# Scores of two groups in one burst, values one tile sooner and a transpose half a tile later, in a fused chunk attention and squared-ReLU FFN on one core

## The chip, the cores and the metric

One Trainium2 chip, of which the kernel uses 1 core. The metric is the device time of one execution in microseconds (us), as the median of several runs. The core's engines run side by side, each with a queue of its own: TensorE (PE) for matmuls and for transposes against an identity, VectorE (DVE), ScalarE (ACT) and GpSimd (POOL) for elementwise work, and SyncE (SP), which issues most DMAs. They wait for each other through semaphores. Loading PE's weights shows as a row of its own, PEld.

## The reference

Attention inside chunks of 64 tokens, for 8 batches, 8 heads, 576 tokens and a head size of 64; then a feed-forward layer with a squared ReLU (d_model 512, d_ff 2048) over all 4608 tokens.

```python
# q_c, k_c, v_c: q, k, v cut into chunks of 64 tokens
scores = scale * np.matmul(q_c, k_c.transpose(0, 1, 2, 4, 3))
scores = scores - np.max(scores, axis=-1, keepdims=True)
attn = np.exp(scores)
attn = attn / (np.sum(attn, axis=-1, keepdims=True) + 1e-09)
out = np.matmul(attn, v_c)
x = np.ascontiguousarray(attn_out.transpose(0, 2, 1, 3)).reshape(B * S, H * D)
h = np.maximum(x @ w_in, 0.0)
return (h * h @ w_out).astype(np.float32)
```

## The kernel before

**Groups and blocks.** 256 tokens (four chunks) are a group; there are 18 groups. Two groups are a block of 512 tokens: block j holds groups 2j and 2j + 1, so block 1 holds groups 2 and 3, and block 4 groups 8 and 9. The feed-forward layer runs block by block, and during block j the attention of block j + 1 is slipped in between. (Block 0 prepares only group 2 of block 1; group 3 is prepared in block 1 itself.) Blocks 0 to 3 (`QUADS = 4`) multiply by w_in in the plain way; from block 4 on, matrix sums save products.

**The attention of a group** has four steps, each a function that issues on several engines.
- q and k are brought into a transposed layout, by PE (`transpose_qk`, L393 with the copies of L402) or, for later groups, cast to bf16 (L442, L447) and transposed by a DMA that SP issues (L453).
- `scores` (`SC`): 32 matmuls of 64 x 64 into one PSUM buffer of two banks (L476), and one ACT exp of 128 x 1024 out of it (L487).
- `values` (`AV`): for each of the group's two token tiles, 16 matmuls of 64 x 65 into a PSUM buffer (L503); a column of ones in v gives the sum of the weights. DVE takes its reciprocal (L435) and multiplies the result by it (L436), writing x.
- `transpose_x` (`XT`): eight PE transposes of x (L533) and one copy from PSUM to `xT` (L538), by ACT for most groups, group 3 among them.

All these take their PSUM buffers from `att_bank`, which in blocks 0 to 3 hands out two buffers by turns, `ps_att` and `ps_att2`. In block 3 the order is: scores 8, scores 9, values 8 (two buffers), values 9 (two), x of 8, x of 9. So the two halves of the values of group 9 write the buffers out of which DVE normalised the two halves of group 8, and PE waits for DVE's last read of each.

**The feed-forward part** is `ffn_in` (L572 to L591). A d_ff tile is 128 rows of d_ff for the tokens at hand: four matmuls into one of four `ps_ffn` buffers, a ReLU by ACT into one of four `relu_sb` buffers (L583), and a square into `gT`, by DVE (L591) or, for the tiles in `SQUARES_ON_ACT = (10, 14, 3)`, by ACT (L589). In blocks 2 and 3 a tile has 512 tokens and 16 tiles follow each other. In block 1 a step is half as wide, 256 tokens: steps 0 to 15 work on group 2 and steps 16 to 31 on group 3, so step 16 is the first to read the x of group 3. `ffn_out` (L773) then multiplies by w_out, with sums by DVE (L607).

**Order.** The schedule is written by hand (`manual_schedule`): each engine runs its instructions in the order in which the program issues them. For blocks 0 to 3 the loop goes through the phases of a block, and each `yield` of a phase ends a slot. Slot s comes behind d_ff tile s (block 1: half tile s); from slot 16 on (block 1: 32) slots lie in `ffn_out`. In a slot, one load is issued if the slot is among `go_slots`, and then whatever `plan` holds for the slot, in the order in which it was put there by `at(slot, f, group)`. The loads of v, q and k go through SP; their slots are in lists of their own, and no load is tied to an attention step's slot.

From block 4 on (`run(tick)`) the order goes by ticks, with lists of the same kind.

Of the kernel before, what the change touches and what calls it, by code (L numbers as in the profile page):

```python
# [144 lines left out]
def kernel(  # L145
# [169 lines left out]
    def go(pieces):  # L315
        for f in pieces:
            f()
# [248 lines left out]
    def ffn_in(j, parts):  # L566
        gT = gT_main.rearrange("p (u h) (f t) -> p u h f t", u=2, f=4)
        xT = xTs[j]
        for u, (c, n, ft) in enumerate((c, n, ft) for c, n, fts in parts for ft in fts):
            h = ps_ffn.tile([128, 512], FP32, name="ps_ffn")  # L570
            for dt in range(n_dt):
                nc.tensor.matmul(  # L572
                    out=h[:, 0:n],
                    lhsT=w_in_bf[:, dt, ft * 128:(ft + 1) * 128],
                    rhs=xT[:, c // 128:(c + n) // 128, dt, :],
                    start=(dt == 0), stop=(dt == n_dt - 1))
            if n == 512 or u % 2 == 0:
                state["rl"] = state.get("rl", -1) + 1
                rl_tile = relu_sb[state["rl"] % 4]
                if j < 3:  # L580
                    rl_tile = rl_tile.bitcast(BF16)
            rl = rl_tile[:, u % 2 * 512:] if n < 512 else rl_tile
            nc.scalar.activation(out=rl[:, 0:n], in_=h[:, 0:n], func=AF.Relu)  # L583
            u0, u1 = c // GT, (c + n) // GT
            dst = gT[:, u0:u1, ft // 4, ft % 4, :]
            src = rl[:, 0:n].rearrange("p (u t) -> p u t", t=GT)
            if (n == 512 and ft in SQUARES_ON_ACT) or (
                    n < 512 and ft in (12, 3)) or (j == 0 and u == 0):
                nc.scalar.activation(out=dst, in_=src, func=AF.Square)  # L589
            else:  # L590
                nc.vector.tensor_tensor(out=dst, in0=src, in1=src, op=ALU.mult)  # L591
            yield
# [16 lines left out]
    def summed(out, in0, in1, op=ALU.add):  # L609
        return lambda *_: add(out, in0, in1, op)  # L610
# [274 lines left out]
    def ffn_out_by_ft(j):  # L885

        n_tt = BT // 128
        o_ps = [ps_ffn.tile([128, d_model], FP32, name="ps_ffn") for _ in range(n_tt)]

        def mm(tt, ft):  # L890
            nc.tensor.matmul(  # L891
                out=o_ps[tt],
                lhsT=g_piece(j, tt // 2, ft // HF, ft % HF // 4)[
                    :, ft % 4, tt % 2 * 128:tt % 2 * 128 + 128],
                rhs=w_out_bf[:, ft, :],
                start=(ft == 0), stop=(ft == n_ft - 1))


        for ft in range(n_ft - 4):
            for tt in range(n_tt - 1 if ft == 0 else n_tt):  # L900
                mm(tt, ft)
                if ft == 1 and tt == n_tt - 2:
                    mm(n_tt - 1, 0)
            yield
        for tt in range(n_tt):
            for ft in range(n_ft - 4, n_ft):
                mm(tt, ft)
            o_sb = ffn_pool.tile([128, d_model], FP32, name="o_sb", bufs=4)
            nc.scalar.copy(out=o_sb, in_=o_ps[tt])
            b, s0 = chunks[blocks[j][tt // 2]][0]  # L910
            t0 = b * S + s0 + tt % 2 * 128
            nc.gpsimd.dma_start(out=out[t0:t0 + 128, :], in_=o_sb)
            yield
# [3 lines left out]
    def pieces(grps):  # L917
        for g in grps:
            yield from qk_pieces(g)
        for g in grps:  # L920
            yield from v_pieces(g)

    SC, AV, XT = scores, values, transpose_x
    TD = transpose_qk_dma
# [71 lines left out]
    for j in range(QUADS):  # L996
        grps, nxt, far = blocks[j], blocks[j + 1], blocks[j + 2]
        plan = {}

        def at(slot, f, *x):  # L1000
            plan.setdefault(slot, []).append((f, x))

        if j == 0:
            loads, go_slots = pieces(far), range(17)
            at(28, summed(b11_p_b21, b11, b21))
            for slot, f in ((24, TA), (27, SC), (29, AV), (31, XT)):
                at(slot, f, nxt[0])
            at(31, TQ, nxt[1])
            at(31, TK, nxt[1])
            at(31, summed(b22_m_b21, b22, b21, ALU.subtract))  # L1010
            phases = [first_ffn_in, ffn_out_by_ft(0)]
        elif j == 1:
            loads, go_slots = itertools.chain(*map(qk_pieces, far)), range(26, 48)
            for slot, f in ((3, SC), (6, AV), (12, XT)):
                at(slot, f, grps[1])
            for i, g in enumerate(nxt):
                for slot, f in ((16 + 4 * i, C), (21 + 4 * i, TD), (36 + i, SC), (38 + 2 * i, AV),
                                (41 + 2 * i, XT)):
                    at(slot, f, g)
            for i, g in enumerate(far):  # L1020
                at(36 + 4 * i, C, g)
                at(42 + 3 * i, TD, g)
            at(2, summed(b12_p_b21, b12, b21))
            at(12, summed(b11_m_b12, b11, b12, ALU.subtract))
            at(20, summed(b12_p_b22, b12, b22))
            out_j = ffn_out(1)
            for i in (20, 27, 29, 31):
                at(i, lambda: next(out_j)())
            phases = [ffn_in(1, [(0, 256, FT_ORDER), (256, 256, FT_ORDER)]), out_j]
        else:  # L1030
            out_j = ffn_out(j)
            for i in (14, 15):
                at(i, lambda: next(out_j)())
            phases = [ffn_in(j, [(0, BT, range(n_ft))])]
            if j == 2:
                loads, go_slots = itertools.chain(*map(v_pieces, nxt), pieces(far)), [
                    *range(16), *range(27, 36)]
                slots = {SC: (6, 10), AV: (12, 22), XT: (15, 28), CQ: (20, 22), CK: (21, 24), TD: (24, 26)}
                for f in (CQ, CK, TD):
                    for i, g in enumerate(far):  # L1040
                        at(slots[f][i], f, g)
                phases.append(out_j)
            else:
                loads, go_slots = pieces(far), range(11)
                at(11, C, far[0])
                at(13, CQ, far[1])
                at(13, TD, far[0])
                slots = {SC: (2, 4), AV: (7, 10), XT: (13, 15)}
            for f in (SC, AV, XT):
                for i, g in enumerate(nxt):  # L1050
                    at(slots[f][i], f, g)
            if j == 2:
                for i, f in enumerate((summed(a21_p_a22, a21, a22),
                                       summed(a12_m_a21, a12, a21, ALU.subtract),
                                       summed(a11_p_a21, a11, a21))):
                    at(1 + 2 * i, f)
        slot = 0
        for phase in phases:
            for _ in phase:
                if slot in go_slots:  # L1060
                    for f in loads:
                        f()
                        break
                for f, x in plan.get(slot, []):
                    f(*x)
                slot += 1
        assert all(x < slot for x in plan), (j, slot, sorted(plan))
        if j < QUADS - 1:
            go(loads)
# [19 lines left out]
    for j in range(QUADS, n_blk):  # L1089
        if j == QUADS:  # L1090
            n = 14 - LEAD
            slots = [1 + 19 * i // n for i in range(n)]
            assert len(slots) == n
        else:
            slots = [s for s in range(4, 20) if s % 16 not in NO_OUT]
# [119 lines left out]
```

## Time and profile before

| | us |
|---|---|
| median of 3 runs | 280.2 (279.85 to 280.92) |
| span of the profiled execution, first to last instruction | 278.3 |
| PE busy | 267.8 |
| PE weight loads (PEld) busy | 206.0 |
| DVE busy | 196.8 |
| ACT busy | 169.8 |
| POOL busy | 91.8 |
| mean granted TensorE clock | 0.999 of full |

One execution was profiled; the profile gives its span, and no time beside it. Times in rows are counted from the first instruction. In a timeline, rows of the same engine, line and tiles that follow without a gap are merged: the row has their start, the time from the first start to the last end, and their count. The ends of matmuls are modelled, and matmuls overlap, so the pace of PE is read from starts. Blocks lie in the trace at 50 to 81 us (block 1), 81 to 110 us (block 2) and 110 to 128 us (the d_ff tiles of block 3).

### The profile page before, as it was taken

The page shows a single profiled execution, that of the slowest core. Times are in us where ns is not written, and L with a number is a line of the kernel's source. Part 1 is how long each engine was busy: PE and PEld are TensorE (multiplying, and loading weights), DVE is VectorE, ACT ScalarE, POOL GpSimd, SP SyncE. Part 2 cuts the span into 40 slices and gives each one's busy share as a digit, 9 for nine tenths or more (in the row PEclk, how much of TensorE's full clock was granted, in tenths as well). Part 3 has the DMA queues.
Part 4 walks back from the last instruction along what each step waited for, and adds up shares of the span by engine and source line. Part 5 has one row for each costly group of instructions (what it writes and reads, how often), then busy time and mean ns, then how long its engine had stood idle before and what let it go on. Part 6 is the DMA issues. An engine that isn't in the chain of part 4 may idle for free.

```text
span 278.3 us, 8007 instructions
## 1 busy us (share of the span) xinstructions
PE 267.8 (96%) x3307; PEld 206.0 (74%) x3307; DVE 196.8 (71%) x365; ACT 169.8 (61%) x301; POOL 91.8 (33%) x124
## 2 busy tenths in 40 slices
PE   2999999999999999999999999999999999999994
PEld 2774454888774588447888888888888888888883
DVE  1266614999438592598989998799779877994751
ACT  1557705895458883868678765566756665756330
POOL 2048832430460012040245234551534312331612
PEclk9999999999999999999999999999999999999999
DMA  7999999999999899997999997798996350310323
GB/s 218 239 345 393 387 325 252 353 205 165 293 190 232 214 205 219 276 239 142 223 228 201 218 245 177 134 201 214 240 187 171 78 59 18 110 43 9 86 67 113
DMA packets 133368, 55.09 MB, mean 198 GB/s; under 512 B 102160, under 2 KB 129040, under 8 KB 133328
## 3 DMA queue, kind: packets, MB, share of 16 engines
q1 hardware_dynamic: 130320, 45.23, 71.3%
q0 software_dynamic: 2864, 9.18, 10.1%
q8 instruction: 27, 0.44, 0.6%
q10 hardware_dynamic: 144, 0.13, 0.1%
q14 instruction: 13, 0.11, 0.1%
HBM read 36.70 MB, written 9.44 MB: 166 GB/s over the span
## 4 chain that ended last, share of the span: by engine, by line
PE 93%; DVE 2%; DMA 2%; ACT 1%; issue 0%; SPq 0%
PE ps_ffn L650 23%; PE ps_out L773 22%; PE ps_ffn L572 18%; PE ps_ffn L773 13%; PE ps_ffn L891 5%; PE ps_att L503 3%; PE ps_att L476 3%; PE ps_att L533 2%; DMA qk_st<-in_k_dram 2%; PE ps_ffn L426 1%; DVE x L436 1%; PE ps_ffn L393 1%; DVE gT L591 1%; PE ps_att L393 1%; PE ps_ffn L514 1%; ACT qkT L402 0%
## 5 line engine op out<-in xcount | busy, mean ns | idle before, releaser
L572 PE MATMUL ps_ffn<-xT,w_in_bf 128*128 128x512 bf16 (+1 forms) x328 | 58.3, 333 | 0.0
L773 PEld LDWEIGHTS <-w_st 128*128 128x128 bf16 x512 | 48.8, 98 | 6.6 <-DVE w_st L607 0.7
L658 DVE CUSTOM_DVE_ANT_0 relu<-ps_ffn,w_st 128x512 f32<-128x512 f32 x60 | 39.2, 684 | 12.8 <-PE ps_ffn L650 11.4
L572 PEld LDWEIGHTS <-w_in_bf 128*128 128x128 bf16 x328 | 31.0, 98 | 21.1
L583 ACT ACTIVATE relu<-ps_ffn 128x256 bf16<-128x256 f32 (+2 forms) x82 | 39.8, 502 | 10.3 <-PE ps_ffn L572 8.6
L591 DVE TENSOR_TENSOR gT<-relu 128x256 bf16<-128x256 bf16 (+2 forms) x68 | 31.9, 500 | 19.9 <-ACT relu L583 19.5
L802 POOL DMA_DIRECT2D out_dram<-o_sb x27 | 19.8, 735 | 54.2 <-DVE o_sb L607 32.4
L650 PE MATMUL ps_ffn<-qk_st,w_in_bf 128*128 128x256 bf16 x240 | 35.3, 273 | 0.0
L650 PEld LDWEIGHTS <-w_in_bf 128*128 128x128 bf16 x320 | 30.7, 98 | 4.0 <-issue 0.2
L773 PEld LDWEIGHTS <-gT 128*128 128x128 bf16 x296 | 28.6, 98 | 3.3
L773 PE MATMUL ps_out<-w_out_bf,w_st 128*128 128x256 bf16 x240 | 30.9, 273 | 0.0
L692 ACT ACTIVATE w_st<-ps_ffn 128x512 f32<-128x512 f32 x20 | 11.9, 597 | 27.5 <-PE ps_ffn L650 27.5
L436 DVE TENSOR_TENSOR x<-ps_att,recs 128x512 bf16<-128x512 f32 x36 | 24.9, 691 | 1.2
L650 PEld LDWEIGHTS <-qk_st 128*128 128x128 bf16 x240 | 22.6, 98 | 2.9
L669 POOL TENSOR_TENSOR qk_st<-relu 128x512 bf16<-128x512 f32 x10 | 10.3, 1035 | 41.6 <-DVE relu L658 38.0
L650 PE MATMUL ps_ffn<-xT,qk_st 128*128 128x256 bf16 x160 | 23.9, 273 | 0.0
L487 ACT ACTIVATE e<-ps_att 128x1024 bf16<-128x1024 f32 x18 | 18.4, 1024 | 8.0 <-PE ps_att L476 8.0
L669 POOL TENSOR_TENSOR gT<-relu 128x512 bf16<-128x512 f32 x10 | 10.3, 1035 | 36.8 <-DVE relu L658 36.8
L667 ACT ACTIVATE gT<-relu 128x512 bf16<-128x512 f32 x28 | 17.7, 632 | 0.0
L773 PE MATMUL ps_ffn<-w_out_bf,w_st 128*128 128x256 bf16 x144 | 17.7, 273 | 0.0
L607 DVE TENSOR_TENSOR w_st<-gT,w_st 128x1024 bf16<-128x1024 bf16 x26 | 17.6, 711 | 0.0
L442 POOL CAST qkb<-qk_st 128x1024 bf16<-128x1024 f32 x12 | 12.7, 1061 | 12.4 <-DMA qk_st<-in_q_dram 12.3
(91 smaller groups left out, 435.7 us busy)
## 6 DMA issues: line engine op xcount, KB each, us to landing
qk_st<-in_q_dram SPq DMA_DIRECT2D x16, 512.0 KB, 5.5
out_dram<-o_sb POOLq DMA_DIRECT2D x31, 256.0 KB, 4.2
qk_st<-in_k_dram SPq DMA_DIRECT2D x24, 256.0 KB, 5.4
ve_sb<-in_v_dram SPq DMA_DIRECT2D x32, 128.0 KB, 4.3
w_st<-in_moe_w_in_dram SPq DMA_DIRECT2D x8, 512.0 KB, 6.4
w_st<-in_moe_w_out_dram SPq DMA_DIRECT2D x8, 512.0 KB, 5.5
vo_sb<-in_v_dram SPq DMA_DIRECT2D x24, 128.0 KB, 3.7
qk_st<-in_k_dram SPq DMA_DIRECT2D x4, 512.0 KB, 6.0
```

The lines of the kernel that those rows point to most:

```text
L436: nc.vector.tensor_tensor(out=x, in0=o[:, :, :, 0:D], in1=rec.to_broadcast([128, 2, n, D]), op=ALU.mult)
L487: nc.scalar.activation(out=e_out, in_=s_in, func=AF.Exp, scale=scale)
L572: nc.tensor.matmul(out=h[:, 0:n], lhsT=w_in_bf[:, dt, ft * 128:(ft + 1) * 128], rhs=xT[:, c // 128:(c + n) // 128, dt, :], start=(dt == 0) ...
L583: nc.scalar.activation(out=rl[:, 0:n], in_=h[:, 0:n], func=AF.Relu)
L591: nc.vector.tensor_tensor(out=dst, in0=src, in1=src, op=ALU.mult)
L607: nc.vector.tensor_tensor(out=out, in0=in0, in1=in1, op=op)
L650: nc.tensor.matmul(out=bank[:, f * GT:(f + 1) * GT], lhsT=a[:, dt, ft * 128:(ft + 1) * 128], rhs=b[:, :, dt, :], start=(first and f == 0 a ...
L658: nc.vector._custom_dve(TENSOR_ADD_SAT, out=out, in0=in0, in1=in1, s0=BIG, s1=0.0)
L667: engine.activation(out=dst, in_=r, func=AF.Square)
L669: engine.tensor_tensor(out=dst, in0=r, in1=r, op=ALU.mult)
L773: nc.tensor.matmul(out=out_ps, lhsT=lhsT, rhs=b[:, i, :], start=(first and i == 0 and (last or t == 0)), stop=(i == HF - 1), skip_group_ch ...
L802: dma.dma_start(out=out[t0:t0 + GT, col:col + HD].rearrange("(t p) d -> p t d", p=128), in_=o_sb.rearrange("p (t d) -> p t d", d=HD))
```

## The change

Four numbers in three lists of slots.

```diff
         elif j == 1:
...
-            for slot, f in ((3, SC), (6, AV), (12, XT)):
+            for slot, f in ((3, SC), (6, AV), (13, XT)):
                 at(slot, f, grps[1])
...
             if j == 2:
...
-                slots = {SC: (6, 10), AV: (12, 22), XT: (15, 28), CQ: (20, 22), CK: (21, 24), TD: (24, 26)}
+                slots = {SC: (6, 6), AV: (12, 22), XT: (15, 28), CQ: (20, 22), CK: (21, 24), TD: (24, 26)}
...
             else:
...
-                slots = {SC: (2, 4), AV: (7, 10), XT: (13, 15)}
+                slots = {SC: (2, 2), AV: (6, 10), XT: (13, 15)}
             for f in (SC, AV, XT):
                 for i, g in enumerate(nxt):
                     at(slots[f][i], f, g)
```

In block 1, the eight transposes of the x of group 3 and their ACT copy are issued behind half tile 13 instead of 12: on PE behind four more matmuls, on ACT behind one more ReLU.

In block 2, the 32 score matmuls of group 7 and their exp follow those of group 6 at once, behind tile 6; they stood behind tile 10. On ACT the exp moves ahead of the ReLUs of tiles 7 to 10 and the square of tile 10.

In block 3, the scores and exp of group 9 follow those of group 8 behind tile 2; they stood behind tile 4. On ACT the exp moves ahead of the ReLUs of tiles 3 and 4 and the square of tile 3. The values of group 8 come behind tile 6 instead of 7: on PE ahead of four matmuls, and on DVE the four instructions that normalise them come ahead of the square of tile 7.

The number of instructions is the same on each engine, and the order on POOL and SP does not change.

## The prediction

> **What bounds the kernel now.** I read the page first, for the span, the engines and the chain that ended last.
>
> ```profile
> span 278.3 us, 8007 instructions
> PE 267.8 (96%) x3307; PEld 206.0 (74%) x3307; DVE 196.8 (71%) x365; ACT 169.8 (61%) x301; POOL 91.8 (33%) x124
> ...
> PEclk9999999999999999999999999999999999999999
> ...
> PE 93%; DVE 2%; DMA 2%; ACT 1%; issue 0%; SPq 0%
> ```
>
> TensorE (PE) is busy for 96% of the span at its full granted clock, and 93% of the chain is its own work. So the time changes only by what the edits do to PE's queue: instructions added, or moments in which PE waits. The edits add none. What is left is found by following PE's queue through the three stretches that the diff touches, in the timeline. There I compare the start of each run of matmuls with the start of the next one. First block 3, which holds two of the four moves. The columns are start, duration, engine, line, operation and count; in brackets is the idle time before it and what ended it.
>
> ```profile
> 110.15 2.75 PE L572 MATMUL ps_ffn<-xT,w_in_bf 128*128 128x512 bf16 x12
> 112.83 0.33 PEld L476 LDWEIGHTS <-qkT 64*64 64x64 bf16 x32 [0.42 <-issue]
> 112.94 0.60 ACT L583 ACTIVATE relu<-ps_ffn 128x512 f32<-128x512 f32 x1 [0.27 <-PE ps_ffn L572]
> 113.21 1.90 PE L572 MATMUL ps_ffn<-xT,w_in_bf 128*128 128x512 bf16 x8
> 113.44 1.02 ACT L487 ACTIVATE e<-ps_att 128x1024 bf16<-128x1024 f32 x1
> 114.34 0.60 ACT L583 ACTIVATE relu<-ps_ffn 128x512 f32<-128x512 f32 x1
> 114.97 0.63 ACT L589 ACTIVATE gT<-relu 128x512 bf16<-128x512 f32 x1
> 115.04 0.33 PEld L476 LDWEIGHTS <-qkT 64*64 64x64 bf16 x32 [0.42 <-issue]
> 115.42 2.76 PE L572 MATMUL ps_ffn<-xT,w_in_bf 128*128 128x512 bf16 x12
> 115.51 0.58 ACT L583 ACTIVATE relu<-ps_ffn 128x512 f32<-128x512 f32 x1
> 117.52 1.29 DVE L591 TENSOR_TENSOR gT<-relu 128x512 bf16<-128x512 f32 x2 [0.71 <-ACT relu L583]
> 118.11 0.34 PEld L503 LDWEIGHTS <-e 64*64 64x64 bf16 x32 [0.42 <-issue]
> 118.50 2.76 PE L572 MATMUL ps_ffn<-xT,w_in_bf 128*128 128x512 bf16 x12
> 118.72 1.04 POOL L442 CAST qkb<-qk_st 128x1024 bf16<-128x1024 f32 x1 [6.77 <-DMA qk_st<-in_q_dram]
> 119.19 1.11 DVE L591 TENSOR_TENSOR gT<-relu 128x512 bf16<-128x512 f32 x1 [0.37 <-ACT relu L583]
> 120.22 0.19 DVE L435 RECIPROCAL recs<-ps_att 128x8 f32<-128x8 f32 x1
> 120.45 0.69 DVE L436 TENSOR_TENSOR x<-ps_att,recs 128x512 bf16<-128x512 f32 x1
> 121.06 0.20 DVE L435 RECIPROCAL recs<-ps_att 128x8 f32<-128x8 f32 x1
> 121.29 0.69 DVE L436 TENSOR_TENSOR x<-ps_att,recs 128x512 bf16<-128x512 f32 x1
> 122.04 0.21 PEld L503 LDWEIGHTS <-e 64*64 64x64 bf16 x16 [0.63 <-DVE x L436]
> 122.30 2.76 PE L572 MATMUL ps_ffn<-xT,w_in_bf 128*128 128x512 bf16 x12
> 124.90 0.61 PE L533 MATMUL ps_att<-ident,x 128*128 128x128 bf16 x8
> 125.34 1.89 PE L572 MATMUL ps_ffn<-xT,w_in_bf 128*128 128x512 bf16 x8
> ```
>
> Call the d_ff tiles of a block t0, t1 and so on, four 512-column matmuls each. Between 122.30 and 124.90 twelve matmuls follow each other without a wait: 2.60 us, so 0.217 us each and 0.867 us a tile. By that pace the twelve from 110.15 are through at 112.75, and the next tile starts at 113.21: the score burst of group 8 costs PE 0.46 us. The burst of group 9 costs 115.42 less 114.95 (113.21 plus eight), 0.47. The values of group 8 cost 118.50 less 118.02, 0.48. The values of group 9 are through only at 122.30, and the tiles before them at 121.10: 1.20 us for the same 32 matmuls. The bracket on the row at 122.04 names the wait: the second half needs the PSUM bank that VectorE (DVE) is still reading for group 8, and that read (L436, from 121.29) ends at 121.98. **This stall is 1.20 - 0.48 = 0.72 us.**
>
> The read is late because DVE squares t5, t6 and t7 ahead of it. The square of t7 takes 1.11 us, where the pair from 117.52 takes 1.29 together. Beside it GpSimd (POOL) casts from 118.72 to 119.76. The square ends 0.54 us after the cast does, although it began at 119.19: it stood still behind the cast.
>
> Next block 1, where the half tiles have 256 columns.
>
> ```profile
> 54.01 2.79 PE L572 MATMUL ps_ffn<-xT,w_in_bf 128*128 128x256 bf16 x24
> ...
> 56.39 0.69 DVE L436 TENSOR_TENSOR x<-ps_att,recs 128x512 bf16<-128x512 f32 x1
> 56.64 0.90 PE L533 MATMUL ps_att<-ident,x 128*128 128x128 bf16 x8
> 56.82 0.42 ACT L589 ACTIVATE gT<-relu 128x256 bf16<-128x256 bf16 x1
> 57.14 0.23 PEld L533 LDWEIGHTS <-x 128*128 128x128 bf16 x4 [0.28 <-DVE x L436]
> 57.14 0.37 ACT L583 ACTIVATE relu<-ps_ffn 128x256 bf16<-128x256 f32 x1
> 57.38 8.46 PE L572 MATMUL ps_ffn<-xT,w_in_bf 128*128 128x256 bf16 x76
> 57.58 1.01 ACT L538 COPY xT<-ps_att 128x1024 bf16<-128x1024 bf16 x1
> ```
>
> Here 24 matmuls take 2.63 us, 0.109 each and 0.44 a half tile. The eight transposes of x of group 3 take 57.38 - 56.64 = 0.74 us; those of group 8 took 125.34 - 124.90 = 0.44. The other 0.30 us is a wait in their middle for DVE's second write of x, which ends at 57.08. What is just as tight shows one row lower. ScalarE (ACT) copies the transposed x from 57.58 to 58.59, and half tile 16, the first that reads it, is twelve matmuls behind 57.38: 58.69.
>
> Last block 2, for the two score bursts.
>
> ```profile
> 87.19 0.34 PEld L476 LDWEIGHTS <-qkT 64*64 64x64 bf16 x32 [0.42 <-issue]
> 87.57 3.63 PE L572 MATMUL ps_ffn<-xT,w_in_bf 128*128 128x512 bf16 x16
> 91.12 0.34 PEld L476 LDWEIGHTS <-qkT 64*64 64x64 bf16 x32 [0.42 <-issue]
> 91.50 1.90 PE L572 MATMUL ps_ffn<-xT,w_in_bf 128*128 128x512 bf16 x8
> ```
>
> Sixteen matmuls from 87.57 end at 91.04, so the burst at 91.12 costs 0.46 us as well. No stall stands in it.
>
> **The change part by part.**
>
> *One burst of 64 in place of two of 32 (blocks 2 and 3).* The same matmuls run, so only entering and leaving a burst can be saved. A burst costs 0.46 to 0.47 us, of which the weight loads of its 32 matmuls take 0.33 (row at 112.83). The trace of before has no burst of 64 scores. From below, the second half costs just its loads, 0.33, and 0.14 is saved; from above it costs a whole burst again and nothing is saved. I take 0.14, since the loads within a burst follow each other without a break and the second set goes to the other PSUM buffer, free since the previous block. **-0.14 us in each of the two blocks.**
>
> What the merged burst does to ACT must be covered. Its queue in block 3 steps from relu to exp in 0.50 us (112.94 to 113.44), from exp to the next in 0.90 (113.44 to 114.34), from relu to its own square in 0.63 and on to the next relu in 0.54. With both exps behind t2: exps at 113.44 and 114.34, relu of t3 at 115.24, its square 115.87, relus of t4, t5, t6 at 116.41, 116.91 and 117.41. Four PSUM buffers serve the tiles, so t7 needs the relu of t3, done at 115.84; t7 comes at 117.49 (below). The 1.65 us between is the cover, and for t8 it is 118.36 - 117.01 = 1.35. If it were gone, each further exp in front would cost PE its 0.90. In block 2 the relu of t6 starts at 87.30 (0.11 behind the burst's first loads, as in block 3), and by the same steps that of t7 ends at 90.2; t11, which wants that buffer, comes at 87.90 + 4 x 0.867 = 91.4. Free as well.
>
> *Values of group 8 behind t6 instead of t7 (block 3).* PE in the new order: t3 at 112.75 + 0.46 + 0.33 = 113.54, t3 to t6 until 117.01, values of group 8 until 117.49, t7 to t10 until 120.96, then the values of group 9. DVE: the relu of t6 is done at 118.01; squares follow every 0.60 (1.29 for two, overlapping by 0.09), so t4 at 117.02, t5 at 117.62, t6 at 118.22; then the same steps as the rows from 120.22, at 118.83, 119.06, 119.67 and 119.90, the last read ending at 120.59. Group 9's second half asks for that bank at about 121.2. The margin is 0.6 us, so the stall goes: **-0.72 us.** From below it might keep all of its 0.72. The square of t7 now runs behind both reads, where nothing on PE waits for it; t11's relu is the next writer of its buffer, after 122.3.
>
> The cast beside DVE is the risk in this term. [...]
>
> *x of group 3 transposed after half tile 13 instead of 12 (block 1).* The transposes start at 56.64 + 0.44 = 57.08, when x is complete, so the 0.30 us wait inside them goes. But the copy behind them has lost half a tile of cover: two half tiles (0.87 us) instead of three stand between the transposes and half tile 16, while the copy takes 1.01. PE would reach half tile 16 at 57.08 + 0.44 + 0.87 = 58.39. The copy cannot start before the transposes are done, 57.08 + 0.61 (row at 124.90) = 57.69, and ACT now has the relu of half tile 13 in front of it: relus at 57.14 and 57.46 (0.32 apart, as from 56.82 to 57.14), copy at 57.78, done at 58.79. Add the 0.06 that stood between x at 57.08 and the load at 57.14: half tile 16 starts at 58.85 instead of 58.69. **+0.16 us.** From below: no wait for the copy at all, -0.30. From above: the relu begins only after its whole 0.37 has passed, and the start costs another 0.1: +0.3. What is queued behind the copy are the relus of half tiles 14 and 15, and PE waits for these only four half tiles on.
>
> **Sum.** +0.16 - 0.14 - 0.14 - 0.72 = -0.84 us on a span of 278.3, so 277.5. The median of the runs shown, 280.2, is 1.9 us over that span, for what lies around it and their spread (279.85 to 280.92); I leave that part as it is: **279.4 us**, 0.3% less. About 0.5% (1.4 us) is what a measurement of this kernel can tell from no change, so this would count as none. Everything after block 3 is the same work in the same order, and moves up with PE; its DMA queues and POOL keep their order.
>
> **The rivals.**
>
> *1. The copy does not hold PE up.* The ends of matmuls are modelled, so the transposes may hand over sooner than 0.61 after they start, and PE's half tile 16 could come at 58.39. Then block 1 gives 0.30 and the sum is -1.30: 278.9. Against it: the copy would have to start at 57.32, ahead of the relu in front of it, and 0.87 of cover is less than 1.01. Chance 0.08.
>
> *2. The stall in block 3 stays.* If the cast begins ahead of the square of t6, DVE stands still until 119.76, and both reads end as in the profile at 121.98; the burst saved before is then lost in the same wait. Net: +0.16 - 0.14, so 280.2. For it: cast and square lie 0.5 us apart (118.72 and 118.22), and the cast starts when a DMA lands. Against it: even with whole durations in place of the steps, ACT finishes t6 at 118.61, still ahead. Chance 0.18.
>
> *3. ACT's backlog makes it slower.* The place is the normalisation of group 8, now behind a square that waits for a relu behind two exps. It decides from the point at which the relu of t6 ends later than about 119.4 (121.98 less the 2.58 from that relu to the end of the second read): 1.4 us beyond my 118.01. Were the backlog 1.9 us longer, group 9 would wait 0.5 us more than now, and the whole is +0.02 + 0.5: 280.7. For it: ACT carries the burst at once, and relu and square of t3 fall right behind. Against it: PE's pace of 0.867 a tile against 0.50 to 0.60 on ACT has the queue nearly caught up at t6 (118.01 against 117.20 if unhindered). Chance 0.10.
>
> **How the numbers follow.** The forecast has 0.55, with a range of its own from 278.9 to 279.9; rivals 1 to 3 have 0.08, 0.18 and 0.10, and 0.09 is for what I don't see, mostly a transfer or a cast that comes at another moment. Eight in ten reach from 278.4 (all gains at their full bounds, and half a microsecond of spread between runs) to 280.9 (rival 3 with a little spread). Faster by over 0.5% (below 278.8): half of rival 1 and the lower tail of the forecast, 0.24. Slower by over 0.5% (above 281.6): what is unseen and the far end of rival 3, 0.12. Between: 0.64.
>
> **What would show it.** In the timeline of the changed kernel: 64 score matmuls in a row with tile starts some 0.79 us apart across them; in block 3 no wait of PE for L436, and 32 value matmuls of group 9 through in 0.48; the square of t6 ahead of POOL's cast; in block 1 no break among the transposes, and instead a gap of about 0.4 us in front of half tile 16, ended by ACT L538. Half tile 16 at or ahead of 58.69 would make the first edit's term wrong, a wait on L436 over 0.2 us the third, and a burst of 64 that costs over 0.9 us the second.

## The result and the profile after

The kernel became slower: 283.29 us as median of 6 runs (282.03 to 285.30), against 279.96 (279.13 to 280.92) for the kernel before; the ratio is 1.0116, 95% interval 1.0087 to 1.0145. The prediction had 279.4, with a range up to 280.9. An execution more than 1.5% above the fastest of its kernel is left out of the ratios, though not out of the medians: one of nine in experiment 1, one of ten in experiment 4 and seven of ten in experiment 9 below. The profiled execution of the changed kernel has a span of 281.4 us and took 283.25, so again about 1.9 us lie around the span. (The instruction count differs from before by matmul records that are missing from the trace; the weight loads are the same 3307.)

First its page: the span, the engines, and the chain that ended last, by engine and by line.

```profile
span 281.4 us, 8005 instructions
PE 266.6 (95%) x3304; PEld 205.0 (73%) x3307; DVE 199.8 (71%) x365; ACT 170.4 (61%) x301; POOL 91.7 (33%) x124
...
PE 81%; DMA 9%; DVE 4%; ACT 2%; issue 1%; POOL 0%; SPq 0%; ACTq 0%
PE ps_out L773 21%; PE ps_ffn L650 20%; PE ps_ffn L572 14%; PE ps_ffn L773 12%; DMA qkT<-qkb 5%; PE ps_ffn L891 5%; DMA qk_st<-in_k_dram 4%; PE ps_att L503 2%; PE ps_att L476 2%; DVE gT L591 2%; PE ps_ffn L426 1%; PE ps_att L533 1%; DVE x L436 1%; ACT relu L583 1%; PE ps_ffn L393 1%
```

PE has 81% of the chain where it had 93%. DMA has 9%, and 5% is one kind of transfer that the chain of before did not have among its large parts: `qkT<-qkb`, the DMA that transposes q and k of a group. The waits of PE in blocks 2 and 3 (engine, line, what it waited for: us in total, times, longest) say where it bites, and the chain in order of time (start, us, what) says why.

```profile
PE ps_att L476 <- DMA qkT<-qkb: 2.9, 1, 2.9
PE ps_att L533 <- DVE x L436: 0.9, 1, 0.9
```

```profile
73.98 7.19 DMA qk_st<-in_k_dram
...
81.23 1.05 POOL qkb L447
...
82.30 7.39 DMA qkT<-qkb
...
89.73 0.45 PE ps_att L476 x32
90.18 5.29 PE ps_ffn L572 x24
```

The last piece of k of group 7 is issued at 73.98 and lands at 81.17, POOL casts it, SP issues the transposing DMA at 82.30, and it lands at 89.69. The scores of group 7 start 0.04 us later. In the timeline they had been ready to go behind the scores of group 6:

```profile
86.41 0.33 PEld L476 LDWEIGHTS <-qkT 64*64 64x64 bf16 x32 [0.42 <-issue]
89.73 0.45 PE L476 MATMUL ps_att<-qkT 64*64 64x64 bf16 x32 [2.88 <-DMA qkT<-qkb]
90.11 5.35 PE L572 MATMUL ps_ffn<-xT,w_in_bf 128*128 128x512 bf16 x24
```

What decided this stood in the profile of before as well, in the view of the tile `qkT`, which the prediction did not use. Its rows give the issues of the DMAs of groups 6 and 7 (durations of the issue, first and last start) and their time to landing:

```profile
L453 SPq DMA_TRANSPOSE qkT<-qkb x2: 3406/3664/3922, 76.1 to 80.2; - x2
DMA to landing us min/median/max: 7.0/7.1/7.2
```

Group 7's was issued at 80.23, as the second of the two issues that the timeline merges into one row from 76.11 to 84.16, and took at most 7.2 us to land: 87.4. Its scores came at 91.13, 3.7 us later. Behind the block's first matmul that is 91.13 - 81.06 = 10.07 us; in the changed kernel they are due when the 0.33 us of group 6's are through, 86.41 + 0.33 - 80.28 = 6.46. So the change brings them forward by 3.6 us and spends nearly the whole slack even of that profile; and in eleven profiles since, all with these loads in the same order, the DMA landed at 87.7 to 91.0. The change did not make it late: in the six profiles that leave block 2 as it was (before and experiments 2, 3, 4, 7 and 11) it landed at 87.4 to 90.1.

By stage, from the first matmul rows of each (us):

| | before | changed | changed, second profile |
|---|---|---|---|
| start to the first d_ff matmul of block 2 | 81.06 | 80.28 | 81.16 |
| block 2, to the first d_ff matmul of block 3 | 29.09 | 31.94 | 30.53 |
| block 3, to the transposes of group 9 | 16.92 | 17.07 | 17.07 |
| the rest | 151.27 | 152.11 | 151.24 |

The first line differs ahead of anything that the edits touch: the 32 transposes that PE starts at about 9.7 us took 1.85 us before, and 1.06 in the first profile of the change. The last line differs mostly by 0.7 us of wait for another group's DMA (group 12), which comes and goes from profile to profile; the second profile of the change has none of it. What the change itself did is 1.4 to 2.9 us in block 2, 0.15 in block 3 and, as shown below, 0.10 in block 1.

In block 3 the value stall is gone, and another wait is there. Timeline of the changed kernel:

```profile
112.22 2.75 PE L572 MATMUL ps_ffn<-xT,w_in_bf 128*128 128x512 bf16 x12
114.90 0.60 PEld L476 LDWEIGHTS <-qkT 64*64 64x64 bf16 x64 [0.42 <-issue]
115.50 1.93 ACT L487 ACTIVATE e<-ps_att 128x1024 bf16<-128x1024 f32 x2
115.54 3.63 PE L572 MATMUL ps_ffn<-xT,w_in_bf 128*128 128x512 bf16 x16
117.31 0.62 ACT L583 ACTIVATE relu<-ps_ffn 128x512 f32<-128x512 f32 x1
119.10 1.90 DVE L591 TENSOR_TENSOR gT<-relu 128x512 bf16<-128x512 f32 x3 [2.77 <-ACT relu L583]
121.99 0.69 DVE L436 TENSOR_TENSOR x<-ps_att,recs 128x512 bf16<-128x512 f32 x1
122.60 3.60 DVE L591 TENSOR_TENSOR gT<-relu 128x512 bf16<-128x512 f32 x3
122.87 1.31 POOL L442 CAST qkb<-qk_st 128x1024 bf16<-128x1024 f32 x1 [8.85 <-DMA qk_st<-in_q_dram]
123.05 0.35 PEld L503 LDWEIGHTS <-e 64*64 64x64 bf16 x32 [0.42 <-DVE x L436]
123.45 2.76 PE L572 MATMUL ps_ffn<-xT,w_in_bf 128*128 128x512 bf16 x12
124.62 1.04 POOL L447 CAST qkb<-qk_st 128x1024 bf16<-128x1024 f32 x1 [0.44 <-DMA qk_st<-in_k_dram]
126.35 0.69 DVE L436 TENSOR_TENSOR x<-ps_att,recs 128x512 bf16<-128x512 f32 x1
127.10 0.62 PE L533 MATMUL ps_att<-ident,x 128*128 128x128 bf16 x8 [0.89 <-DVE x L436]
```

The values of group 9 go through without a break (123.05 to 123.45). But the three squares behind the normalisation of group 8 take 3.60 us, where three took 1.90 in the same block: two GpSimd casts lie beside them. So DVE normalises group 9 late, until 127.04 for its first half, and the transposes of group 8 at 127.10, the next user of that PSUM buffer, wait 0.89. By the starts they come 1.05 us late, as the twelve matmuls from 123.45 are through at 126.05.

In block 1:

```profile
53.13 3.23 PE L572 MATMUL ps_ffn<-xT,w_in_bf 128*128 128x256 bf16 x28
56.20 0.61 PE L533 MATMUL ps_att<-ident,x 128*128 128x128 bf16 x8
56.65 1.04 PE L572 MATMUL ps_ffn<-xT,w_in_bf 128*128 128x256 bf16 x8
56.85 1.01 ACT L538 COPY xT<-ps_att 128x1024 bf16<-128x1024 bf16 x1
57.91 1.36 PE L572 MATMUL ps_ffn<-xT,w_in_bf 128*128 128x256 bf16 x11 [0.23 <-ACT xT L538]
```

The transposes take 0.45, without the break, and half tile 16 waits for the copy that ends at 57.86.

### The profile page after: what moved, and what is told of

The parts are those of the page before. It is cut to its first block, busy times and chain, and to the rows that moved or that the text cites. A ratio compares the mean times of both kernels' runs of the same rounds, so it can differ in the third digit from the quotient of the medians.

```text
span 281.4 us, 8005 instructions
## 1 busy us (share of the span) xinstructions
PE 266.6 (95%) x3304; PEld 205.0 (73%) x3307; DVE 199.8 (71%) x365; ACT 170.4 (61%) x301; POOL 91.7 (33%) x124
## 4 chain that ended last, share of the span: by engine, by line
PE 81%; DMA 9%; DVE 4%; ACT 2%; issue 1%; POOL 0%; SPq 0%; ACTq 0%
PE ps_out L773 21%; PE ps_ffn L650 20%; PE ps_ffn L572 14%; PE ps_ffn L773 12%; DMA qkT<-qkb 5%; PE ps_ffn L891 5%; DMA qk_st<-in_k_dram 4%; PE ps_att L503 2%; PE ps_att L476 2%; DVE gT L591 2%; PE ps_ffn L426 1%; PE ps_att L533 1%; DVE x L436 1%; ACT relu L583 1%; PE ps_ffn L393 1%
## 5 line engine op out<-in xcount | busy, mean ns | idle before, releaser
L591 DVE TENSOR_TENSOR gT<-relu 128x256 bf16<-128x256 bf16 (+2 forms) x68 | 34.3, 542 | 20.7 <-ACT relu L583 20.4
L442 POOL CAST qkb<-qk_st 128x1024 bf16<-128x1024 f32 x12 | 13.8, 1148 | 15.4 <-DMA qk_st<-in_q_dram 15.3
```

## The experiments

Each edit is against the kernel before unless it says otherwise. Two theories were set against each other. **Landing**: the burst in block 2 asks for group 7's q and k before their DMA has landed. **Backlog**: two exps in a row hold ScalarE up, in both blocks alike. Times are medians; ratios are to the kernel before on the same chip, with their 95% intervals. They are not quotients of the medians shown; the medians of the kernel before were 280.1 to 280.4 us there.

**1. Block 2 alone.**

```diff
-                slots = {SC: (6, 10), AV: (12, 22), ...
+                slots = {SC: (6, 6), AV: (12, 22), ...
```

> Only the burst in block 2 (scores 6 and 7 both behind tile 6). Landing theory: scores 7 now come about 3.6 us sooner, which is all the slack that the transposing DMA of group 7 had before (landed 87.41, scores 91.13, so 3.72), so PE waits for that DMA in block 2: 0 to 3 us by when the loads come, and this part alone gives most of the 3.3 us (ratio 1.005 to 1.012). Backlog theory (two exps in a row on ScalarE hold everything up, in both blocks alike): no DMA wait in front of scores 7, ratio at most 1.003.

282.05 us, ratio 1.0069 (1.0035 to 1.0103). PE's waits in block 2, and the stretches of the same execution (busy time of PE, PEld, DVE, ACT, POOL with counts, granted clock, DMA):

```profile
PE ps_att L476 <- DMA qkT<-qkb: 2.5, 1, 2.5
```

```profile
84.00:88.00 4.00, 4.00 (x20) 1.71 (x18) 3.48 (x6) 3.42 (x6) 1.83 (x3) 1.00 0.80 170
88.00:92.00 4.00, 1.54 (x67) 0.95 (x67) 1.90 (x3) 1.85 (x3) 0.00 (x0) 0.90 0.95 245
92.00:96.00 4.00, 4.00 (x14) 1.58 (x13) 0.82 (x2) 2.03 (x4) 0.00 (x0) 0.67 0.81 181
96.00:100.00 4.00, 4.00 (x50) 1.83 (x48) 1.79 (x6) 2.94 (x6) 0.00 (x0) 1.00 1.05 262
```

As the landing theory had it: 2.5 us of wait for that DMA, from this edit alone. The second fence shows something that neither theory had: behind the wait the granted clock is below full, 0.90 in the stretch from 88 us, which holds the wait, and 0.67 in the next. This execution took 285.90, the longest of its nine; three of the nine had a mean clock of 0.992 or less.

**2. Block 3 alone.**

```diff
-                slots = {SC: (2, 4), AV: (7, 10), XT: (13, 15)}
+                slots = {SC: (2, 2), AV: (6, 10), XT: (13, 15)}
```

> Only the moves in block 3 (scores 8 and 9 behind tile 2, values 8 behind tile 6). Landing theory: the DMA of group 9 lands 5 us ahead of its scores, so no DMA wait here; the value stall of 0.72 goes, 0.18 is saved by the burst, and up to 1.05 comes back in front of the transposes of group 8 when a GpSimd cast stops the squares on VectorE: ratio 0.997 to 1.001. Backlog theory: the block gets slower, ratio 1.004 or more.

279.37 us, ratio 1.0008 (0.9982 to 1.0034), no wait for a DMA in block 3. Block 3 took 16.34 us to the transposes of group 9, 0.58 less than before, with 0.2 of the new wait left. The backlog theory's 1.004 lies outside the interval.

**3. Block 1 alone.**

```diff
-            for slot, f in ((3, SC), (6, AV), (12, XT)):
+            for slot, f in ((3, SC), (6, AV), (13, XT)):
```

> Only the transpose of group 3 behind half tile 13. By the trace of the changed kernel 0.30 is gained inside the transposes and 0.39 lost in front of half tile 16: ratio 1.000 to 1.001, with the wait for the ScalarE copy in the trace. Rival (the copy hides): ratio 0.999 and half tile 16 without a gap.

280.69 us, ratio 1.0032 (1.0001 to 1.0062): more than expected, though the expected 1.000 to 1.001 is in part inside the interval. Timeline around the transposes:

```profile
54.01 3.23 PE L572 MATMUL ps_ffn<-xT,w_in_bf 128*128 128x256 bf16 x28
57.57 0.23 PEld L533 LDWEIGHTS <-x 128*128 128x128 bf16 x4 [0.27 <-DVE x L436]
57.80 1.04 PE L572 MATMUL ps_ffn<-xT,w_in_bf 128*128 128x256 bf16 x8
59.07 1.14 PE L572 MATMUL ps_ffn<-xT,w_in_bf 128*128 128x256 bf16 x9 [0.23 <-ACT xT L538]
```

The gap in front of half tile 16 is there (1.27 us from 57.80 for eight matmuls of 0.87). The break within the transposes stayed too, as x came 0.4 us later than in the profile of before, so nothing was gained in exchange: half tile 16 comes 5.06 us behind 54.01, where it came 4.68 behind. That is 0.38 of some 0.9; 0.3 more, in this profile, is again a wait for group 12's DMA, and the interval, 0.0 to 1.7 us, leaves room for the rest to be noise. In experiment 4, with the same edit, x came in time and half tile 16 stood 4.77 behind.

**4. The change without block 2** (the edits of 2 and 3 together).

> The changed kernel with the old slots in block 2 (6 and 10). Landing theory: the loss goes, ratio 0.997 to 1.002. Backlog theory: about half of the loss stays, ratio about 1.006. A third reading, that the loss is the loads' lateness by chance and no part of the change, expects here too a wait of PE for a transposing DMA of a microsecond or more.

280.19 us, ratio 1.0011 (0.9983 to 1.0038), with no wait for a transposing DMA in blocks 2 and 3. Undoing one number takes the loss away. The backlog's 1.006 lies outside; so does chance as the cause, as the DMA did not land early here: issued at 81.93, it took 7.4 us and landed at 89.3, later than the 89.2 of experiment 12, where PE waited 1.5 us for it. Only the reader stood elsewhere.

The parts do not add up to the whole exactly: 0.69% in experiment 1 for block 2 and 0.11% here for the rest make 0.80%, where the change cost 1.16%. The intervals are wide enough to hold that, and no run shows whether something is left.

**5. Scores 7 sooner, but no burst.**

```diff
-                slots = {SC: (6, 10), AV: (12, 22), ...
+                slots = {SC: (6, 8), AV: (12, 22), ...
```

> Block 2 only, scores 7 two tiles sooner (behind tile 8 instead of 10) and no burst. Landing theory: what counts is when scores 7 come, so PE asks 1.73 us later than with the burst behind tile 6; the DMA landed between 6.3 and 9.4 us behind the block's first matmul in the runs so far, and scores 7 come at 8.4, so the wait is 0 to 1 us: ratio 1.000 to 1.005. Backlog theory (two exps in a row): without a burst no loss at all and no wait, ratio 1.000.

280.97 us, ratio 1.0032 (1.0005 to 1.0060). PE's waits in block 2:

```profile
PE ps_att L476 <- DMA qkT<-qkb: 1.1, 1, 1.1
```

About half of the loss of experiment 1 without any burst: it is the moment at which scores 7 ask that costs.

**6. A burst, but late.** `SC: (9, 9)` in the same line.

> Block 2 only, both scores in one burst behind tile 9. Landing theory: scores 7 come at about 9.2 us behind the block's first matmul, at or behind the landing, so the burst costs nothing and saves its 0.18: ratio 0.998 to 1.001, wait for the DMA under 0.3 us. Backlog theory: the burst itself costs, ratio 1.004 or more.

280.52 us, ratio 1.0008 (0.9973 to 1.0042). The DMA landed about 0.3 us before its scores; no wait. So with scores 7 behind tile 6, 8, 9 and 10, PE waited 1.5 to 2.9, 1.1, 0 to 0.2 (the 0.2 in experiment 8) and 0 us, with and without a burst. The saving of the burst itself does not show in the ratio, whose interval does not exclude the backlog theory's 1.004 either. In this profile the 64 matmuls cost 0.69 us, where two bursts of before cost 0.93; but PE then came sooner to the transposes of group 6's x, which DVE finished no sooner (at 96.5 in both profiles), and they took 0.75 us in place of 0.48.

**7. Block 3 with the transposes of group 8 a tile later**, `SC: (2, 2), AV: (6, 10), XT: (14, 15)`, to cover the new wait.

> The moves of block 3 and x of group 8 transposed behind tile 14 instead of 13. If the transposes wait for the PSUM buffer of the values of group 9, which VectorE normalises late behind squares that a GpSimd cast stops, one tile (0.87 us) covers the 0.33 to 1.05 seen: wait under 0.2, ratio 0.996 to 0.999. If they wait for x of group 8 itself or for the ScalarE backlog, a tile later changes nothing in the sum: ratio as without it, 1.000.

279.97 us, ratio 0.9996 (0.9967 to 1.0024). The wait in front of the transposes went, and came back behind them (timeline, first matmuls of `ffn_out`):

```profile
127.44 1.91 PE L773 MATMUL ps_out<-w_out_sum,gT 128*128 128x256 bf16 x16 [0.55 <-ACT xT L538]
```

The output's PSUM buffers lie where `ps_att2` was, and its first matmul waits for the ACT copy of group 8's x, which now comes later. The expectation missed: one tile of cover was bought for 0.55 us of wait.

**8. Both together**, `SC: (9, 9)` in block 2 and the line of experiment 7 in block 3, block 1 as before.

> The moves of block 3 with the transposes of group 8 behind tile 14, and the burst of block 2 behind tile 9; block 1 as before. Landing theory: 0.7 to 1.1 us less than before, ratio 0.996 to 0.998. Backlog theory: slower than before, 1.004 or more.

280.43 us, ratio 1.0003 (0.9970 to 1.0037). No faster than before within the interval; the 0.55 us of wait in front of `ffn_out` is there as in experiment 7.

**9. The burst behind tile 6, with group 6's loads ahead of group 5's transposing DMA in SP's queue.**

```diff
-            loads, go_slots = itertools.chain(*map(qk_pieces, far)), range(26, 48)
+            loads, go_slots = itertools.chain(*map(qk_pieces, far)), range(23, 48)
...
-                slots = {SC: (6, 10), AV: (12, 22), ...
+                slots = {SC: (6, 6), AV: (12, 22), ...
```

> The burst in block 2 behind tile 6 as in the change, nothing else of it; and in block 1 the three loads of q and k of group 6 go ahead of group 5's transposing DMA in SP's queue instead of behind it. Landing theory: what follows in that queue, group 7's transposing DMA at its end, lands 1 to 3 us sooner, so the wait in front of scores 7 shrinks from 2.6 to 2.9 us to under 1.5 although the burst stands where it stood; group 5's DMA lands later and scores 5 wait for it in block 1, 1 to 3 us. Backlog theory: nothing about block 2 changes, its wait stays above 2 us.

286.28 us, ratio 1.0120 (1.0068 to 1.0172). Waits in blocks 1 and 2, and stretches around them:

```profile
PE ps_att L476 <- DMA qkT<-qkb: 5.7, 1, 5.7
```

```profile
72.00:76.00 4.00, 0.00 (x0) 0.00 (x0) 0.00 (x0) 0.00 (x0) 1.66 (x2) 0.95 1.22 209
76.00:80.00 4.00, 3.09 (x73) 2.18 (x74) 0.18 (x1) 1.02 (x1) 1.04 (x1) 0.50 1.56 293
```

The one wait is that of scores 5 in block 1, now 5.7 us, far over the expected 1 to 3, with a granted clock of 0.95 and 0.50 in the two stretches. In block 2 there is none. But that does not prove what it was meant to: group 7's DMA landed at 86.7, 2.5 us or more sooner than in the other profiles with the burst behind tile 6, and PE came some 7 us later, and either is enough.

**10. The same early loads without the burst.**

> The same early loads without the burst (scores 7 behind tile 10): the control. Landing theory: no wait in block 2, the same wait of scores 5 in block 1, so the ratio is that wait alone, 1.003 to 1.010; e9 and this one differ by less than 0.005, where the burst alone cost 0.007.

287.30 us from four runs, ratio 1.0262 (1.0223 to 1.0300), with 5.1 us of wait for scores 5. The expected size was missed a second time. The two ratios differ by more than the expected 0.005, and the kernel without the burst is the slower one; that of experiment 9 rests on three of its ten executions, and the medians differ by 1.0 us in the same order. So the pair decides nothing.

**11. Of block 3 only the values.**

```diff
-                slots = {SC: (2, 4), AV: (7, 10), XT: (13, 15)}
+                slots = {SC: (2, 4), AV: (6, 10), XT: (13, 15)}
```

> Block 3 only, and of its moves only the values of group 8 (behind tile 6); its scores stay behind tiles 2 and 4. If the value stall is VectorE's place for the normalisation, it goes without the burst too: no wait of PE for L436 in front of the values of group 9, ratio 0.997 to 0.999. If the stall went because of the earlier exp of group 9, it stays, ratio 1.000.

280.22 us, ratio 0.9996 (0.9973 to 1.0019), span of the profiled execution 277.5. Timeline around the values of group 9:

```profile
117.44 1.29 DVE L591 TENSOR_TENSOR gT<-relu 128x512 bf16<-128x512 f32 x2 [0.71 <-ACT relu L583]
119.72 0.69 DVE L436 TENSOR_TENSOR x<-ps_att,recs 128x512 bf16<-128x512 f32 x1
120.33 2.87 DVE L591 TENSOR_TENSOR gT<-relu 128x512 bf16<-128x512 f32 x3
121.11 0.35 PEld L503 LDWEIGHTS <-e 64*64 64x64 bf16 x32 [0.42 <-issue]
```

The second read ends at 120.41, 0.70 before the values start; no wait of PE is left in block 3, which takes 16.23 us to the transposes of group 9, 0.69 less than before. The stall goes without the earlier exp. In the time of whole runs 0.25% does not stand out.

**12. The change once more.**

> The whole change once more, unaltered, for a second profile of it. Landing theory: again a wait of PE of 2 to 4 us for the transposing DMA of group 7 in front of scores 7, ratio 1.007 to 1.015; where the wait is near 3 us and more, a stretch of half clock behind it as in the first experiment, 1.5 us more. Reading by chance (the loads of the first profile came late by accident): a wait under 1 us in this profile and a ratio under 1.005.

283.02 us from four runs (281.81 to 284.96), ratio 1.0123 (1.0064 to 1.0183). PE's waits in blocks 2 and 3:

```profile
PE ps_att L476 <- DMA qkT<-qkb: 1.5, 1, 1.5
PE ps_att L533 <- DVE x L436: 0.9, 1, 0.9
```

The wait is there again, shorter than expected; so it is no accident of one execution, and its length moves with the landing. The expectation's 3 us, from which a stretch of half clock was to follow, was the author's estimate, and the runs do not bear it out: the clock fell behind 2.5 us of wait in experiment 1 and stayed at 1.00 behind 2.9 us in the first profile of the change.

## Why the prediction was wrong

**The step that failed** is the one-burst term: "the second set goes to the other PSUM buffer, free since the previous block", and, of block 2, "Free as well". It checked what the burst writes and what comes behind it on ScalarE, and did not check what the moved instruction reads. Scores 7 read `qkT` of group 7, which a DMA writes. The view of that tile had the numbers: landed at 87.4, read at 91.1. Moving the reader 3.6 us forward left 0.1 us of that slack, and cost almost every bit by which the DMA came later than in that one profile: 1.5 and 2.9 us in the two profiles of the change, in place of a gain of 0.14. Experiments 1, 4, 5 and 6 show this by doing it alone, undoing it, and halving it.

The sentence "its DMA queues and POOL keep their order" was true, and no protection: with the loads in one and the same order this DMA landed between 87.4 and 91.0 us. A transfer that comes late stood in the prediction only among "what I don't see, mostly a transfer or a cast that comes at another moment", with 0.09.

**The wait itself, 1.5 to 2.9 us, is not all of 3.3.** The time behind it is argued, not shown in the profiles of the change: in the first the granted clock is 1.00 in every stretch from 80 to 112 us, and in the second block 2 took 1.44 us more than before, no more than its wait of 1.5. In experiment 1 the clock is not full, and the clocks of the whole runs fit: of the ten runs of the change, the six with a mean clock of 0.994 or less took 283.0 to 285.3 us, the other four 281.8 to 283.3. Only two of the ten have a profile, so where the others lost clock is not shown.

**Block 1** was right in mechanism and near in size. Half tile 16 came 57.91 - 53.13 = 4.78 us behind the start of its stretch, against 4.68 before: +0.10 for the predicted +0.16, with a gap of 0.39 for the predicted 0.4. Experiment 3 as a whole measured more than this term, but its interval holds the term too.

**The burst** costs what was worked out, or less: twelve matmuls from 112.22 end at 114.82 and the next tile starts at 115.54, 0.72 for 64 matmuls where 0.79 was predicted and two bursts cost 0.93.

**ScalarE's backlog and the values of group 8** came out nearly to the hundredth. Block 3 began 2.07 us later than in the profile of before. With that added, the relu of t3 was due at 117.31 and came at 117.31; the second read of group 8 was due to end at 122.66 and ended at 122.68. The 0.72 us of value stall went. Rival 3, a backlog longer than worked out, fell.

**What came in its place in block 3** is rival 2's mechanism at a place that the prediction did not cover, and it is the second step that failed: block 3 was to gain 0.86 us and lost 0.15. The first cast, from 122.87, caught neither the square of t6 nor that of t7, which began at 122.60 and took 0.68 us; the casts caught those of t8 and t9, now behind the normalisation. The prediction had it that for the square of t7 "nothing on PE waits"; in truth the normalisation of group 9 is queued behind these squares, and the transposes of group 8 need the buffer that it empties. That cost 1.05 us, more than the 0.72 of the stall and the 0.21 of the burst that were won. The three squares took 3.60 us beside two casts and 1.90 without. That of t8 began at 123.20, 0.33 behind the first cast, took 1.52 and ended 0.54 behind the cast's end at 124.18; that of t9 began at 124.64, 0.02 behind the second, took 1.55 and ended 0.53 behind its end at 125.66. In the profile of before the square of t7 ended 0.54 behind its cast as well. The first cast itself lasted 1.31, the second 1.04. How much comes back moves with the casts: in experiment 2 the three squares took 2.88 us and PE waited 0.2, in experiment 4 they took 3.08 and it waited 0.4. In experiment 11 they took 2.87, PE came to the transposes a little later, as it still had two bursts to pay for, and nothing came back.

**Rival 1**, the copy that hides, fell: half tile 16 waited for it.

## What to carry to other kernels

Before an instruction is moved ahead, list what it reads, and for each operand that a DMA brings subtract landing from first use in the trace: that slack, less how much the landing varies from run to run, is how far it may move. A saving in an engine that is busy for 96% of the span has to be set against the longest wait that it can open on that engine, as the two differ by more than a factor of ten here (0.2 against 2.9 us). And after a stall is removed, follow the queue of the engine that caused it one more step: who is behind, and whose buffer it empties.

## What the runs showed of the hardware that was not expected

**A wait of PE cost more than its length in experiment 1.** PE stood there for 2.5 us, and the granted clock was 0.90 in the stretch from 88 us, which holds the wait, and 0.67 in the next. That is 4 x 0.10 + 4 x 0.33 = 1.7 us of clock lost, or about 3.4 us at half speed, on top of the wait. The starts agree: the 24 matmuls from 91.53 took 6.7 us, 1.5 more than at 0.217 each, and the weight loads from 91.94 to 94.50 start 0.43 us apart, at half that pace. In experiment 9, after 5.7 us, the mean clock of the stretch from 76 us was 0.50. In the first profile of the change, after 2.9 us, the clock stayed at 1.00, so the length of the wait alone does not decide, and no run shows what does.

**Landing times of one and the same DMA moved by 3.6 us.** In the twelve profiles with the loads in the old order, the transposing DMA of group 7 landed between 87.4 and 91.0, though SP's queue and what it moves are the same in all. Against that spread a slack of a microsecond or two, read from one profile, is none.
